# Moving weight conversions, key norms and block reads to other pieces of the first period of a DeltaNet + maxout-FFN kernel

## The chip, the cores and the metric

The kernel runs on one core of a Trainium2 chip. The metric is the device time of one execution in microseconds (us), lower is better. A core has a matrix engine (PE, with its weight loads listed as PEld), a vector engine (DVE), a scalar engine (ACT), a general engine (POOL) and SP, which here only issues DMA transfers. Each engine works through its own instruction list strictly in order and waits on semaphores for the others.

## The reference

Two blocks follow each other. The first is a DeltaNet recurrence over 768 tokens for 4 batches and 8 heads of 48 dimensions; the second is a feed-forward block whose hidden layer is the maximum of three projections.

```python
k_n = k / (np.linalg.norm(k, axis=-1, keepdims=True) + 1e-06)
for t in range(S):
    kt, vt, bt = (k_n[:, :, t], v[:, :, t], beta[:, :, t, None])
    y[:, :, t] = np.einsum('bhd,bhde->bhe', q[:, :, t], state)
    v_old = np.einsum('bhde,bhd->bhe', state, kt)
    state = state + bt[:, :, :, None] * np.einsum('bhd,bhe->bhde', kt, vt - v_old)
...
x = y.transpose(0, 2, 1, 3).reshape(B * S, H * D)          # 3072 x 384
h = np.maximum(np.maximum(x @ w1, x @ w2), x @ w3)         # 3072 x 768
return h @ w_out                                           # 3072 x 384
```

Everything is float32 at the outside; the inputs of the weights arrive as 64-bit floats, which the kernel reads as pairs of 32-bit words and turns into float32 itself.

## The kernel before

**Tiling.** The recurrence is done in 12 chunks `c` of 64 tokens. A *unit* `n = 2c + g` is one chunk for two of the four batches. Two chunks make a *period* `m` (4 units, 512 rows of x); there are 6 periods. Per unit, `turn` (L330) transposes keys and queries on PE (`p_t`) and copies them to `kqt`; `gram` (L400) multiplies keys by keys and by queries (`p_g`), of which DVE takes the masked query part `pt` (L395) and ACT the key part `at` (L428); `to_dram` (L432) writes `at` to DRAM (`at_d`). `blocks(m)` (L461) reads a period's four sets of 32x32 diagonal blocks back from DRAM with four DMAs (L471), so that each partition holds one whole block (`x_bl`; for period 1 it lies inside the tile `wo_sb`).

**The triangular solve.** `solve(m)` (L481) is a generator that runs almost wholly on DVE: it clears `y_bl` (L489), scales by the key norms (`norm`, L243, and L493 to L505) and then does column after column of an elimination, each one product (L519, `tmp`) and one subtraction (L523, `y_bl`). For periods 0 and 1 there are 15 columns of 16x16 blocks, later 31 columns of 32x32 blocks. Then it stores the result to DRAM (L528, `y_d`) and reads it back into `ut` (L537). Each resumption (`some(solving, k)`) does k columns. The chunk recurrence follows: `halves_t`/`halves_z`/`halves_u` (`p_e`, `p_f`), `join_z`/`join_u` (`p_z`, `p_j`), `old_k`/`old_q`, `new` (`p_u`), `step` (`p_s`, state `st` at L731), `to_y` and `to_x` (`p_x`, then the copy into `xt`, L805 to L808).

**Norms of the values.** `prep_sums(c)` (L260) squares the keys on ACT (L267), sums them on DVE (L268) and swaps halves with two small DMAs (L273). `prep_values(c)` (L282) turns the sums into norms (one square root on ACT, L245, five small DVE instructions, L246 to L250) and scales `v_t` on POOL (L277).

**Weights.** There are 24 slabs: 18 of w1 to w3 (in the order in which the hidden pieces need them) and 6 of w_out. `fetch` (L188) queues a slab's DMA (L192) into one of 5 `w_bits` buffers. One call of `some(conv, 1)` converts: ACT takes `mant` (L211) and `up` (L220) of a new slab, POOL clamps `mant` (L215), and the slab of the call before is joined: DVE L230 and L234, then a POOL addition (L238) into `w_sb` or `wo_sb`. `mant` and `up` have two buffers each. The same five buffers later hold `turned`, the keys and queries that `load_blocks` (L358) brings straight from DRAM.

**The feed-forward generator.** `ffn(m)` (L811) yields after each *piece*. In period 0, pieces 0 to 8 are the first 256 columns of hidden rows 0 to 2, pieces 9 to 17 the other 256 columns, pieces 18 to 26 hidden rows 3 to 5 with 512 columns, each 3 matmuls into `p_h` (2 PSUM buffers) and one take-over: piece 0, 3, 6, ... by ACT (L830), the two others by DVE (L832, `h`). Pieces 27 to 30 are the outputs `p_o`, copied by ACT (L854) and stored by SP (L857). Piece i needs the buffer of piece i-2 to be free. PE work of the recurrence shares three PSUM buffers in turn (`ps_two`).

**Order.** Nothing is scheduled by a planner: within `manual_schedule` each engine's list is the order in which the Python code calls. The loop at L1019 goes through the pieces of `ffn(0)`, and after each piece emits the rest of period 0 (`FIRST`), the work on period 1 (`EARLY_LINKS`), conversions (`CONVERTED`), loads, norms, and the solves of periods 1 and 2. Later periods use the loop at L1060. DMAs go to SP's queue in the same order; one whose data or buffer isn't ready holds up all behind it.

Of the kernel before, what the change touches and what calls it, by code (L numbers as in the profile page):

```python
# [21 lines left out]
def kernel(  # L22
# [31 lines left out]
    nc = tc.nc  # L54
# [47 lines left out]
    one_queue = (nc.sync, nc.sync)  # L102
# [355 lines left out]
    def in_blocks(t):  # L458
        return t[:, :, 0 : HB * BL].rearrange("p s (j i) -> p s j i", i=BL)

    def blocks(m, queues=one_queue):  # L461
        if m == 1:
            xs[m] = in_wo(0)
        else:
            xs[m] = work.tile([128, 2, HB * BL + HB], FP32, name="x_bl", bufs=1)
        x = in_rows(xs[m])
        for half in range(2):
            part = slice(BL * half, BL * (half + 1))
            for cc in range(2):
                p0 = 64 * half + 32 * cc  # L470
                queues[cc].dma_start(  # L471
                    out=x[p0 : p0 + 32],
                    in_=at_d[m][cc, part, :, :, part].rearrange(
                        "j b h i -> (b h) j i"
                    ),
                )
# [4 lines left out]
    def solve(m):  # L481
# [3 lines left out]
        if m == 1:  # L485
            y_bl = in_wo(1)
        else:
            y_bl = work.tile([128, 2, HB * BL + HB], FP32, name="y_bl", bufs=1)
            (nc.vector if m else nc.gpsimd).memset(y_bl, 0.0)  # L489
        y = in_rows(y_bl)  # L490
        bl = small("bl", BL)
        norm(bl, diagonal(x), small("root_bl", BL), small("nt_bl", BL))
# [83 lines left out]
    fine = {}  # L576
# [23 lines left out]
        return slice(hs[0], hs[-1] + 1)  # L600

    def halves_z(c):
        if c not in fine:
            halves_t(c)
        at = [ats[2 * c + g] for g in range(2)]
        second = ut[c % NU].rearrange("p g h (f two x) -> p g h f two x", two=2, x=HB)
        for hs, p_v, copy in heads_of(c, "p_e", BL):
            for i, h in enumerate(hs):
                for bb, g in TILES:
                    r = rows(bb)  # L610
                    nc.tensor.matmul(
                        p_v[rows(bb ^ g), g, i], at[g][r, h], second[r, g, h, :, 1]
                    )
            copy(zs[c % NU][:, :, span(hs)], p_v)
# [247 lines left out]
    def some(gen, n):  # L862
        for _ in range(n):
            if next(gen, gen) is gen:
                break
# [86 lines left out]
    halves_z(1)  # L952
    load_q(3)
    to_x(0)
    for n in range(2):
        some(conv, 1)
        fetch(nc.sync)
    load_q(4)
    load_v(2)
    solving = solve(1)  # L960
    some(solving, 2)

# [50 lines left out]

    CONVERTED = {4, 5, 6, 7, 8, 10, 12, 14, 16, *range(17, 27)}
    for i, _ in enumerate(ffn(0)):  # L1019
        if i > 4 and i - 1 in CONVERTED:  # L1020
            fetch(nc.sync)
        queries(FIRST.get(i, ""))
        links(1, EARLY_LINKS.get(i, ""))
        if i in CONVERTED:
            some(conv, 1)
        if i in (1, 2):
            prep_sums(i + 1)
        if i in (4, 5):
            some(solving, 4 if i == 4 else 2)
        if i in (5, 7):  # L1030
            prep_values(i // 2)
        if i in (5, 6, 9, 10):
            load_k(i + 3 - i // 9 * 2)
        if i == 0:
            load_v(3)
        if i == 12:
            load_q(11)
        if i in (15, 18):
            load_v(4 + i // 18)
        if i == 19:  # L1040
            blocks(2)
            prep_sums(4)
        if i == 20:
            solving = solve(2)
            some(solving, 1)
        if i > 20:
            some(solving, 3 if i < 29 else 4)
        if i == 21:
            prep_values(4)
        if i == 22:  # L1050
            prep_sums(5)
        if i == 24:
            prep_values(5)
        if i in (27, 28):
            load_blocks(i - 15)

# [47 lines left out]
```

## Time and profile before

| | |
|---|---|
| median of 4 runs | 591.69 us (590.99 to 592.17) |
| profiled execution: own time, span | 592.17 us, 590.5 us |
| granted PE clock, mean over the span | 0.948 |
| PE busy | 543.1 us (92%), 8106 matmuls |
| DVE busy | 348.0 us (59%), 778 instructions |
| ACT busy, POOL busy | 140.3 us (24%), 119.0 us (20%) |
| chain that ended last, by engine | PE 61%, DVE 13%, DMA 10%, SP queue 6% |

The profile is of one execution, the slowest of the four shown. "Busy" is an average over stages with different limits, so the stage that the change touches has to be read by itself. Pieces 0 to 30 of `ffn(0)` lie between 61.3 us and 194.5 us of the span: piece 9 starts at 99.4, piece 18 at 132.6, piece 27 at 176.4. In a row of the timeline the numbers are start and duration in us, then engine, line, instruction, output and inputs, count, and in brackets the idle time of the engine before it and what ended it.

### The profile page before, as it was taken

What the parts mean: (1) busy time and instruction counts of PE and PEld (TensorE: products, weight loads), DVE (VectorE), ACT (ScalarE), POOL (GpSimd) and SP (SyncE); (2) the same over time, 40 slices, a digit from 0 to 9 for tenths busy, and PEclk for the clock granted to TensorE, in tenths of its full rate; (3) what the DMA queues carried; (4) which work ended last, traced back from release to release, by engine and by line L of the source; (5) the groups of instructions that cost most, each with busy time, mean ns of one, the idle gap of its engine ahead of it and who ended that gap; (6) DMA issues with size and microseconds to landing.
All of it is one profiled execution on the core that took longest, in us unless ns stands there. A gap on an engine that the chain in (4) does not pass through costs nothing.

```text
span 590.5 us, 18712 instructions
## 1 busy us (share of the span) xinstructions
PE 543.1 (92%) x8106; PEld 318.7 (54%) x8106; DVE 348.0 (59%) x778; ACT 140.3 (24%) x274; POOL 119.0 (20%) x209
## 2 busy tenths in 40 slices
PE   6468699999869999999999999999999999999997
PEld 5337577775435545555555455455455455554443
DVE  1648879766799453899554898555895432201110
ACT  3326336545311122112121112121111211010000
POOL 6024206213326423002802004600001000000000
PEclk9556779999998999999999999999999999999999
DMA  9998916967204654264754644833744101210002
GB/s 159 154 173 227 195 25 137 190 156 157 47 2 116 145 117 101 73 118 95 185 120 82 115 90 109 190 86 73 119 101 92 17 2 54 68 40 1 0 0 53
DMA packets 159505, 58.76 MB, mean 100 GB/s; under 512 B 141184, under 2 KB 153280, under 8 KB 159424
## 3 DMA queue, kind: packets, MB, share of 16 engines
q1 hardware_dynamic: 150736, 51.58, 42.8%
q0 software_dynamic: 3200, 4.82, 3.5%
q10 hardware_dynamic: 5488, 1.18, 1.2%
q8 instruction: 63, 1.03, 0.8%
q14 instruction: 18, 0.15, 0.1%
HBM read 40.21 MB, written 17.30 MB: 97 GB/s over the span
## 4 chain that ended last, share of the span: by engine, by line
PE 61%; DVE 13%; DMA 10%; SPq 6%; issue 3%; ACT 3%; POOL 2%; ACTq 0%; DVEq 0%; POOLq 0%
PE p_h L822 38%; PE p_o L846 9%; DVE y_bl L523 3%; PE p_g L411 3%; DMA y_d<-y_bl 3%; DMA kpad<-in_k_dram 3%; DVE tmp L519 2%; SPq L369 2%; PE p_u L703 2%; PE p_k L675 1%; PE p_t L339 1%; PE p_j L658 1%; DMA ut<-y_d 1%; SPq L115 1%; PE p_q L675 1%
## 5 line engine op out<-in xcount | busy, mean ns | idle before, releaser
L822 PE MATMUL p_h<-xt,w_sb 128*128 128x512 f32 (+1 forms) x702 | 303.8, 577 | 7.0 <-ACT h L830 2.8
L822 PEld LDWEIGHTS p_h<-xt,w_sb 128*128 128x128 f32 x702 | 129.3, 193 | 129.9 <-issue 116.0
L832 DVE TENSOR_TENSOR h<-h,p_h 128x512 f32<-128x512 f32 (+1 forms) x78 | 50.1, 642 | 94.4 <-PE p_h L822 93.7
L846 PE MATMUL p_o<-wo_sb,h 128*128 128x384 f32 x288 | 96.1, 494 | 3.8 <-DVE h L832 3.8
L846 PEld LDWEIGHTS p_o<-wo_sb,h 128*128 128x128 f32 x288 | 55.2, 193 | 42.1 <-issue 6.0
L523 DVE TENSOR_TENSOR y_bl<-y_bl,tmp 128x31 f32<-128x31 f32 (+20 forms) x139 | 57.7, 415 | 4.8
L277 POOL TENSOR_TENSOR v_t<-v_t,nrm 128x768 f32<-128x768 f32 x12 | 17.7, 1474 | 193.3 <-DVE nrm L250 165.1
L369 POOL DMA_DIRECT2D turned<-in_q_dram x96 | 52.1, 550 | 4.2 <-POOL turned L364 3.8
L519 DVE TENSOR_TENSOR tmp<-x_bl,y_bl 128x31 f32<-128x31 f32 (+20 forms) x139 | 47.3, 340 | 3.7
L830 ACT COPY h<-p_h 128x512 f32<-128x512 f32 (+1 forms) x39 | 21.5, 552 | 106.2 <-PE p_h L822 106.2
L411 PE MATMUL p_g<-kqt 48*64 48x64 f32 (+1 forms) x1280 | 34.2, 250 | 10.4 <-ACT kqt L345 5.7
L411 PEld LDWEIGHTS p_g<-kqt 48*64 48x64 f32 x1280 | 28.5, 148 | 19.5 <-ACT kqt L345 7.9
L854 ACT COPY o_sb<-p_o 128x384 f32<-128x384 f32 x24 | 11.5, 478 | 91.4 <-PE p_o L846 80.1
L215 POOL TENSOR_SCALAR mant<-mant 128x384 f32<-128x384 f32 x24 | 12.5, 520 | 72.1 <-ACT mant L211 71.4
L428 ACT COPY at<-p_g 128x512 f32<-128x512 f32 x21 | 12.3, 585 | 45.3 <-DVE pt L395 40.1
L395 DVE TENSOR_TENSOR pt<-p_g,mask 128x512 f32<-128x512 f32 x22 | 15.2, 690 | 10.3 <-PE p_g L411 10.1
L385 DVE STREAM_TRANSPOSE kqt<-turned 128x256 f32<-128x256 f32 x48 | 17.3, 415 | 4.9 <-DMA turned<-in_k_dram 4.7
L238 POOL TENSOR_TENSOR w_sb<-mant,up 128x384 int32<-128x384 int32 x18 | 18.0, 999 | 5.5 <-DVE mant L234 5.5
L618 DVE TENSOR_SCALAR ut<-p_j 32x512 f32<-32x512 f32 (+1 forms) x13 | 8.3, 647 | 17.6 <-ACT ut L620 17.6
L703 PEld LDWEIGHTS p_u<-v_t,ut 64*64 64x64 f32 x768 | 13.4, 142 | 8.4 <-issue 5.1
L731 DVE TENSOR_TENSOR st<-st,p_s 128x768 f32<-128x768 f32 x11 | 10.5, 950 | 12.4 <-PE p_s L725 12.3
L675 PEld LDWEIGHTS p_k<-st,kqt 48*64 48x64 f32 x704 | 12.0, 140 | 9.9 <-issue 6.9
(111 smaller groups left out, 488.9 us busy)
## 6 DMA issues: line engine op xcount, KB each, us to landing
w_bits<-in_moe_w_dram SPq DMA_DIRECT2D x18, 384.0 KB
at_d<-at SPq DMA_DIRECT2D x45, 128.0 KB
v_t<-in_v_dram SPq DMA_DIRECT2D x24, 192.0 KB
turned<-in_q_dram POOLq DMA_DIRECT2D x96, 48.0 KB, 3.2
out_dram<-o_sb SPq DMA_DIRECT2D x48, 96.0 KB
turned<-in_k_dram SPq DMA_DIRECT2D x96, 48.0 KB
kpad<-in_k_dram SPq DMA_DIRECT2D x44, 96.0 KB
y_x<-y SPq DMA_DIRECT2D x16, 192.0 KB
```

Source lines behind the costliest of these rows:

```text
L238: nc.gpsimd.tensor_tensor(out=dst.bitcast(I32), in0=mant_v.bitcast(I32), in1=up_v, op=ALU.add)
L277: nc.gpsimd.tensor_tensor(out=vts[c], in0=vts[c], in1=nrm[:, :, :, None].to_broadcast([128, 2, H, D]), op=ALU.mult,)
L369: (nc.sync, nc.gpsimd)[i].dma_start(out=t[p0 : p0 + 32, bb, at : at + NP * 2 * D].rearrange("p (j x) -> p j x", j=NP), in_=(k, q)[i][2 * b ...
L411: nc.tensor.matmul(p_g[rows(bb ^ (g * i)), par, c0 : c0 + C * (1 + whole)], kq[:, 0], kq if whole else kq[:, i],)
L519: nc.vector.tensor_tensor(out=t_v, in0=row.to_broadcast(t_v.shape), in1=column.to_broadcast(t_v.shape), op=ALU.mult,)
L523: nc.vector.tensor_tensor(out=rest, in0=rest, in1=t_v, op=ALU.subtract)
L675: nc.tensor.matmul(p_b[rows(bb), par, c0 : c0 + D], kqt[g][dims(par), j, bb ^ g, i], st[dims(par), bb ^ g, g, j],)
L703: nc.tensor.matmul(p_v[rows(bb ^ g), g, i], ut[c % NU][rows(bb), g, h], rhs[rows(bb), g, h],)
L822: nc.tensor.matmul(p_h, w_sb[i][:, t, f * 128 : (f + 1) * 128], xt[:, t, lo : lo + w], start=(t == 0), stop=(t == KT - 1),)
L830: nc.scalar.copy(h, p_h)
L832: nc.vector.tensor_tensor(out=h, in0=h, in1=p_h, op=ALU.max)
L846: nc.tensor.matmul(p_o, hs[f][:, i * 128 : (i + 1) * 128], wo_sb[:, f], start=(f == 0), stop=(f == FT - 1),)
```

## The change

Only the order of work before and during `ffn(0)` is changed, and one engine.

- Two weight conversions and two fetches that stood ahead of the loop are gone from there, and so is one of the two resumptions of `solve(1)`. The 19 conversion calls in the loop (pieces 4 to 8, 10, 12, 14, 16, 17 to 26) become 20 (2 to 8, 10, 12 to 23). The last slab is joined at piece 22 and not 24; each fetch still stands one piece behind a conversion.
- `halves_t(1)`, three DVE transposes (L583, L585), is no longer called in `halves_z(1)` ahead of `to_x(0)` but behind it. So DVE's half of the copy into `xt` (L808) now precedes them.
- `solve(1)` does 4, 2 and 1 steps at pieces 4, 5 and 6 and not 4 and 2 at 4 and 5: its store moves from piece 4 to 5 and its second reload to piece 6.
- Key loads for units 8 to 11 move from pieces 5, 6, 9, 10 to 7 to 10; a load of v from piece 15 to 10.
- The sums for chunks 4 and 5 move from pieces 19 and 22 to 11 and 15, their norms from 21 and 24 to 14 and 20.
- `blocks(2)` is issued in two parts: chunk 0's two DMAs at piece 16, chunk 1's two at piece 18, and not all four at 19.
- `solve(2)` starts at piece 21 and not 20, does 3 steps at pieces 22 to 26, 4 at 27 to 29 and 5 at 30 (before: 3 at 21 to 28, 4 at 29 and 30). Its `y_bl` is cleared by POOL and not by DVE.

```diff
-    def blocks(m, queues=one_queue):
+    def blocks(m, queues=one_queue, chunks=(0, 1)):
         if m == 1:
             xs[m] = in_wo(0)
-        else:
+        elif m not in xs:
             xs[m] = work.tile([128, 2, HB * BL + HB], FP32, name="x_bl", bufs=1)
...
-            for cc in range(2):
+            for cc in chunks:
...
-            (nc.vector if m else nc.gpsimd).memset(y_bl, 0.0)
+            (nc.vector if m > 2 else nc.gpsimd).memset(y_bl, 0.0)
...
     def halves_z(c):
-        if c not in fine:
+        if c > 1:
             halves_t(c)
...
     to_x(0)
-    for n in range(2):
-        some(conv, 1)
-        fetch(nc.sync)
+    halves_t(1)
     load_q(4)
     load_v(2)
     solving = solve(1)
-    some(solving, 2)
+    some(solving, 1)
...
-    CONVERTED = {4, 5, 6, 7, 8, 10, 12, 14, 16, *range(17, 27)}
+    CONVERTED = {*range(2, 9), 10, *range(12, 24)}
     for i, _ in enumerate(ffn(0)):
-        if i > 4 and i - 1 in CONVERTED:
+        if i - 1 in CONVERTED:
             fetch(nc.sync)
...
-        if i in (4, 5):
-            some(solving, 4 if i == 4 else 2)
+        if i in (4, 5, 6):
+            some(solving, (4, 2, 1)[i - 4])
         if i in (5, 7):
             prep_values(i // 2)
-        if i in (5, 6, 9, 10):
-            load_k(i + 3 - i // 9 * 2)
+        if 7 <= i < 11:
+            load_k(i + 1)
...
-        if i in (15, 18):
+        if i in (10, 18):
             load_v(4 + i // 18)
-        if i == 19:
-            blocks(2)
-            prep_sums(4)
-        if i == 20:
+        if i in (11, 15):
+            prep_sums(4 + i // 15)
+        if i in (14, 20):
+            prep_values(4 + i // 20)
+        if i in (16, 18):
+            blocks(2, chunks=(i // 18,))
+        if i == 21:
             solving = solve(2)
             some(solving, 1)
-        if i > 20:
-            some(solving, 3 if i < 29 else 4)
-        if i == 21:
-            prep_values(4)
-        if i == 22:
-            prep_sums(5)
-        if i == 24:
-            prep_values(5)
+        if 21 < i < 27:
+            some(solving, 3)
+        if i >= 27:
+            some(solving, 4 if i < 30 else 5)
         if i in (27, 28):
             load_blocks(i - 15)
```

## The prediction

> **What bounds the kernel now.** First I read the table of slices, then the waits of PE by stretch, then the timeline of PE and DVE side by side. In the slices, 40 of 14.8 us each:
>
> ```profile
> PE   6468699999869999999999999999999999999997
> DVE  1648879766799453899554898555895432201110
> PEclk9556779999998999999999999999999999999999
> ```
>
> Beyond slice 14 PE is full; what can be had lies in the first 13. The change touches slices 4 to 13. Busy times there by stretch (engine, busy us, instructions; then granted clock, DMA share and GB/s):
>
> ```profile
> 66.80:82.00 15.20, 10.85 (x246) 8.77 (x245) 11.46 (x30) 4.67 (x12) 0.00 (x0) 0.66 0.82 106
> 82.00:97.00 15.00, 14.46 (x367) 11.84 (x366) 13.80 (x38) 8.40 (x18) 5.00 (x6) 1.00 0.39 88
> 97.00:111.00 14.00, 14.00 (x363) 11.63 (x361) 13.25 (x25) 7.84 (x15) 7.03 (x8) 1.00 0.75 159
> 111.00:132.50 21.50, 19.44 (x599) 16.11 (x599) 13.60 (x28) 10.39 (x21) 3.58 (x6) 1.00 0.83 164
> 146.00:176.40 30.40, 23.28 (x302) 11.90 (x298) 26.35 (x63) 7.67 (x17) 8.61 (x10) 0.94 0.16 29
> ```
>
> The reader is to see three kinds of stretch: DVE full from 82 to 111 (27.05 of 29 us), DVE with room from 111 to 132.5 (13.6 of 21.5), and DVE full again from 146 to 176 (26.35 of 30.4) while PE loses 7 us. PE's waits, first from 57 to 97, then from 145 to 200:
>
> ```profile
> PE p_z L645 <- DVE ut L618: 1.8, 1, 1.8
> ...
> PE p_x L757 <- DVE st L731: 0.5, 1, 0.5
> ```
>
> ```profile
> PE p_o L846 <- DVE h L832: 3.8, 1, 3.8
> PE p_h L822 <- DVE h L832: 2.6, 2, 1.9
> PE p_h L822 <- ACT h L830: 0.7, 1, 0.7
> ```
>
> So in the second place PE stands for DVE's take-over of the hidden pieces, which waits in DVE's list behind the solve, conversions and norms. Two rows of PE show that a stall costs twice, for the next matmuls run at half clock (2.84 and 7.91 us are what the same rows take undisturbed); the DVE rows show a step of the solve beside a POOL addition and the next one without:
>
> ```profile
> 159.89 4.51 PE L822 MATMUL p_h<-xt,w_sb 128*128 128x512 f32 x6 [1.93 <-DVE h L832]
> ...
> 176.43 9.67 PE L846 MATMUL p_o<-wo_sb,h 128*128 128x384 f32 x24 [3.78 <-DVE h L832]
> ```
>
> ```profile
> 161.97 0.99 DVE L523 TENSOR_TENSOR y_bl<-y_bl,tmp 128x112 f32<-128x112 f32 x1
> 162.99 0.30 DVE L519 TENSOR_TENSOR tmp<-x_bl,y_bl 128x135 f32<-128x135 f32 x1
> ```
>
> **The change part by part.** PE's own list is the same before and after; only its waits can move. All times are places in the old trace.
>
> *1. The start of the loop (58 to 97).* DVE's copy of `xt` stood behind three transposes (58.60 to 60.75) and ended at 61.19. Ahead of them it still waits for ACT's half (to 60.27), so it ends at 60.3 + 0.52 = 60.8: 0.4 us. The transposes then end near 63.0, ahead of their reader `p_f` at 63.8. Two joins (61.22 to 63.71, 2.5 us) leave DVE, and with them the ACT conversion that held `root_bl` until 64.47. The norm of `solve(1)` can start at 63.0 and, as its first step took 0.97 beside POOL where 0.18 is usual, takes 2.85 and not 3.6 us. Then the second L618 ends at 67.5 (before 69.96), `p_z` starts at 67.9 (70.11) and `p_k` at 68.6 (71.09): 2.5 us won by PE.
>
> It does not keep them. The two joins (1.9 us) come back at pieces 2 and 3, and one solve column (0.45) comes behind that L618, in a stretch where DVE is the bound. From the first L618 (68.67) to the end of `st` (95.63) DVE was busy 23.5 us and waited 3.5. Now it starts at 66.15, has 23.5 + 1.9 + 0.45 = 25.85 us of work, and I find 2.4 us of waits left (0.44 for ACT's half of L618, 0.6 for squares, 1.3 for `p_j`): `st` ends at 94.4. Adding 0.6 for one more POOL addition beside it (0.99 against 0.30 above) gives 95.0. `p_x`, which takes over the PSUM buffer that `st` frees, gains 0.6 to 1.2; I take 0.9. From `st` to 111 DVE's list is unchanged and full, so 0.9 is what arrives at 111. Bounds: 2.5 (all kept) and -1.7: PE now stands some 2 us in small pieces between 87 and 95, and 1.93 us of standing ahead of 159.89 was followed by 1.67 of half clock.
>
> The Trainium skill's "TensorE: Matmul & The Clock Gate", in its table on why this matters, wants gaps under about 3 us for the clock to stay up; by that rule the -1.7 would be nil. The row with 1.93 decides against it here.
>
> *2. The middle (111 to 146).* DVE gets two more joins (0.95 each), chunk 4's norm (1.0) and chunk 5's sums (1.0), 3.9 us, less a clearing of 0.94; ACT gets two more conversions (1.0 each). The room is there (DVE 7.9 us from 111 to 132.5), but lists are in order. Laid out: the join of piece 13 and a `z` copy behind ACT's conversion push `pt` at 123.69 by 1.0; ACT's `at` follows that, then its conversion, a root (0.2), `h`, `z`, and `kqt`, which ends at 129.1 and not 127.56. `p_g` at 128.43 waits for it: 0.7. Squares and a conversion then precede L620/L618, and `p_t` at 131.64 finds its buffer freed 0.4 later. That is -1.1. By 140 both engines have caught up. Bounds: 0, and -5.6 if the 3.9 us are all exposed, with one spell of half clock (1.7). A gain isn't excluded: three gaps of PE put down to "issue" here, 2.1 us in all, may go, for the loads move too.
>
> *3. The wait for DVE (146 to 186).* Of four joins behind the norm (0.94, 2.09, 0.95, 0.95) one is left (0.95); chunk 5's sums (1.0) and two norms (1.05, 1.07) leave; and five solve steps that ran 0.7 to 0.95 us too long beside POOL (0.94 for 0.22, 0.99 for 0.26, 1.02 for 0.33, 1.08 for 0.38, 1.37 for 0.42) have one POOL addition left beside them. DVE loses 7.1 us of work and some 3 of slowing (3.8 less one 0.7). In the new order, with the norm at 151.95 (below), `h` of piece 22 comes at 155.2 (before 159.06), needed by PE at 157.3; piece 23's at 159.1, needed at 161.1; piece 25's ends at 165.65, needed at 167.7; piece 26's at 169.0, needed at 171. `h` of piece 21 no longer stands on ACT behind `root_bl`. All four waits go: 0.73 + 1.93 + 0.71 + 3.78 = 7.15, and with them the half clock, 4.51 - 2.84 = 1.67 and 9.67 - 7.91 = 1.76 (stall inside `p_o` included). Together 10.6. Bounds: 10.6, and 5.0 if piece 23's margin of 2 us fails and one stall with half clock stays, or two of 1 us.
>
> *4. Blocks by chunk.* Four L471 issues took 6.62 us of SP behind unit 11's `at_d`; now two (3.3) precede it, which with a pair of L273 (1.2) and two fetches (1.3) makes `at_d` 1.2 later, and two follow. `x_bl` lands near 150.5 (151.1), but ACT's `root_bl` now stands behind `qs` and a conversion, so the norm starts at 151.95 (151.48). I cost it at nothing: DVE has `h` and joins until 149.95. If chunk 0's issues stood for data, at worst another 3.3 us on `solve(2)`, whose end has 1.2 to spare (5). The other SP moves, key loads behind fetches, land near 107.4 (issue end 102.6 plus the 4.8 that the chain shows at 28.83) for `p_t` at 108.7: 0, at worst 0.7.
>
> *5. The end of `solve(2)`.* It matters, for `p_z` at 213.93 already waits 0.69 for `ut`. Before, columns ended at 193.34, but SP issued the store at 196.31, behind the output of piece 30 (`p_o` ends 194.5). After: 169.9, plus 2.7 for three columns, plus 12.1 for 16 (181.23 to 193.34): 184.8, against `p_o` ending at 184.1 and the store's turn at 186. So the store follows PE still, and the gain passes on. Lost cover costs one for one.
>
> *6. Clearing by POOL.* It takes 0.94 from DVE at 148.08, where DVE waited afterwards: nothing. By the Trainium skill's "SBUF — State Buffer", section on who interferes with whom, a POOL instruction that only writes doesn't block DVE's two-input steps; no row of this trace has such a pair, and a reading one cost 0.7.
>
> **Sum.** 0.9 - 1.1 + 10.6 = 10.4. Against the profiled execution's own 592.17: 581.8. The median of the runs is 0.5 lower; I leave that inside the scatter.
>
> **The rivals.**
>
> *Half of it (20%).* DVE stays the bound from 146 on: `h` of piece 23 or 25 comes 2 us late, a stall and a half-clock spell stay, or the solve ends 3 to 5 us behind the store's turn. For it: DVE is still over 80% full there. Against: the margins in 3 are all over 1 us. 5 us less: 587.
>
> *No change (5%).* The gain is handed back at `p_z`, because `ut` is late. For: the wait is there now. Against: SP's store follows PE. It needs columns that end 11 us after 184.8. 592.
>
> *Slower (12%).* ACT stands at L211 for POOL's addition of two slabs earlier, which stands for a DVE join; with eight conversions at pieces 12 to 19, each holds up the copies of `z`, `kqt` and `ut` that PE waits for next. For it: ACT waits this way 12.4 us in all before, up to 3.3 at a time. Against: only 21.4 of 35 us of ACT are used. It decides from 10.4 / 8 = 1.3 us per conversion, on top of the 1.1 in part 2; at 1.7 the time is 595.
>
> *More (3%).* The 2.3 us gap at 72.85 and the "issue" gaps go too: 577.
>
> **How the numbers follow.** The forecast, 578 to 586, has 60%. The range reaches to most of the half case: 578 to 589.5. A change of 0.2% is 1.2 us, about what a measurement of this kernel can tell. Faster: 60 + 20 + 3 = 83%; same 5%; slower 12%.
>
> **What would show it.** Right: no wait of PE for `h` between 146 and 186, clock 1.0 there; `p_x` near 95 and `p_z` near 68; waits near 129 of about 1 us; the store of `y_d` right behind piece 30's output. Wrong: `kqt` or `z` over 2 us late near 129, or `p_z` after the loop waiting several us for `ut`.

## The result and the profile after

The changed kernel takes 589.25 us (median of 33 runs, 584.16 to 594.78) beside 592.49 us for the kernel before on the same chips: a ratio of 0.9936, 95% interval 0.9918 to 0.9954. It is faster by 0.64%, 3 to 4 us, where 10.4 us were forecast. The profiled execution has an own time of 589.13 us and a span of 587.4 us (before: 592.17 and 590.5).

The three lines of the slices, of the kernel after:

```profile
PE   6358797979999999999999999899999999999997
DVE  1548789776899553898554897455895422301110
PEclk9556789998999999999999999899999999999999
```

The dip of PE in the eleventh and twelfth digits (148 to 177 us) is gone, so the place at which most of the gain was forecast did change. Now the busy times by stretch, of the kernel after (start:end, length; busy us and instructions of PE, weight loads, DVE, ACT, POOL; granted clock, DMA share, GB/s):

```profile
66.80:82.00 15.20, 13.21 (x349) 10.80 (x348) 11.88 (x31) 5.97 (x13) 0.51 (x1) 0.78 0.36 61
82.00:97.00 15.00, 10.75 (x258) 8.45 (x257) 14.31 (x34) 7.57 (x16) 6.68 (x8) 1.00 0.56 136
97.00:111.00 14.00, 13.32 (x360) 11.13 (x360) 12.92 (x25) 7.00 (x14) 7.38 (x10) 1.00 0.83 166
111.00:132.50 21.50, 17.05 (x502) 14.13 (x499) 15.35 (x33) 11.48 (x25) 5.18 (x8) 1.00 0.76 162
146.00:176.40 30.40, 29.93 (x504) 16.84 (x504) 26.66 (x57) 6.90 (x14) 18.25 (x31) 1.00 0.29 59
```

Read the PE column against the one before. From 146 to 176 us PE is busy 29.93 us (before 23.28) at a clock of 1.00 (0.94). From 66.8 to 82 it is busy 13.21 us where it was 10.85, work that comes sooner. But from 82 to 97 it is busy 10.75 us where it was 14.46, and from 111 to 132.5 17.05 where it was 19.44: time that came in at the end went out in front. PE's waits, of the kernel after, from 57 to 97 us (first fence), 97 to 145 (second) and 145 to 200 (third); total us, times, longest:

```profile
PE p_g L411 <- DVE y L745: 2.1, 1, 2.1
...
PE p_x L757 <- DVE st L731: 1.1, 1, 1.1
```

```profile
PE p_g L411 <- DVE z L649: 2.7, 1, 2.7
...
PE p_t L339 <- DMA kpad<-in_k_dram: 0.6, 2, 0.5
```

```profile
PE p_h L822 <- DVE h L832: 0.5, 1, 0.5
```

The wait of `p_z` for `ut` (1.8) is gone, and of 7.1 us of waiting behind 145 us one of 0.5 is left. New is a wait of `p_g` for the copy `z`, and behind it two rows at half clock (1.10 and 1.56 us are what they take undisturbed):

```profile
132.94 1.74 PE L411 MATMUL p_g<-kqt 48*64 48x128 f32 x32 [2.65 <-DVE z L649]
134.61 2.56 PE L822 MATMUL p_h<-xt,w_sb 128*128 128x256 f32 x6
```

The two PE rows that stood at half clock before are these in the kernel after (start, us, engine):

```profile
159.81 2.84 PE L822 MATMUL p_h<-xt,w_sb 128*128 128x512 f32 x6
...
174.05 8.01 PE L846 MATMUL p_o<-wo_sb,h 128*128 128x384 f32 x24
```

2.84 and 8.01 us against 4.51 and 9.67: full clock, no wait. And the solve step that took 0.99 us beside POOL, with the step behind it:

```profile
167.42 0.28 DVE L523 TENSOR_TENSOR y_bl<-y_bl,tmp 128x112 f32<-128x112 f32 x1
167.73 0.30 DVE L519 TENSOR_TENSOR tmp<-x_bl,y_bl 128x135 f32<-128x135 f32 x1
```

From PE's timelines I cut the span at three marks: the first `p_x` of the loop, the start of `p_h` of piece 18 (the first piece 512 tokens wide), and the end of `p_o` of piece 30. Lengths in us:

| stretch | before | after | gain | forecast |
|---|---|---|---|---|
| start to `p_x` | 95.69 | 96.62 | -0.93 | +0.9 |
| `p_x` to `p_h`(18) | 36.88 | 42.10 | -5.22 | -1.1 (and part 4: 0) |
| `p_h`(18) to end of `p_o`(30) | 61.95 | 51.76 | +10.19 | +10.6 |
| from there to the end | 395.98 | 396.92 | -0.94 | 0 |
| sum | 590.5 | 587.4 | +3.1 | +10.4 |

So the question is not why DVE's wait stayed (it went) but what took 6 us away in front of it. In the middle stretch, from `p_x` to `p_h`(18), PE's own rows account for 5.0 of the 5.2 us: its waits sum to 5.5 us where they were 2.1, and the two rows at half clock take 1.6 us more.

### The profile page after: what moved, and what is told of

The parts are those of the page before. It is cut to its first block, busy times and chain, and to the rows that moved or that the text cites. A ratio compares the mean times of both kernels' runs of the same rounds, so it can differ in the third digit from the quotient of the medians.

```text
span 587.4 us, 18714 instructions
## 1 busy us (share of the span) xinstructions
PE 541.9 (92%) x8106; PEld 318.5 (54%) x8106; DVE 348.6 (59%) x777; ACT 139.4 (24%) x274; POOL 120.0 (20%) x210
## 4 chain that ended last, share of the span: by engine, by line
PE 69%; DVE 11%; DMA 9%; issue 3%; SPq 3%; ACT 3%; POOL 1%; ACTq 0%; DVEq 0%; POOLq 0%
PE p_h L822 42%; PE p_o L846 11%; DMA kpad<-in_k_dram 4%; PE p_g L411 4%; DVE tmp L519 2%; DVE y_bl L523 2%; PE p_y L743 2%; PE p_k L675 2%; DMA turned<-in_q_dram 2%; PE p_u L703 2%; PE p_s L725 1%; SPq L115 1%; PE p_q L675 1%; PE p_j L658 1%; PE p_t L339 1%
## 5 line engine op out<-in xcount | busy, mean ns | idle before, releaser
L846 PE MATMUL p_o<-wo_sb,h 128*128 128x384 f32 x288 | 94.4, 487 | 0.0
L523 DVE TENSOR_TENSOR y_bl<-y_bl,tmp 128x31 f32<-128x31 f32 (+20 forms) x139 | 54.9, 395 | 4.8
L267 ACT ACTIVATE ksq<-kpad 128x384 f32<-128x384 f32 x20 | 9.9, 519 | 31.8 <-DMA kpad<-in_k_dram 31.5
```

The costliest lines, as they stand in the source:

```text
L523: nc.vector.tensor_tensor(out=rest, in0=rest, in1=t_v, op=ALU.subtract)
L846: nc.tensor.matmul(p_o, hs[f][:, i * 128 : (i + 1) * 128], wo_sb[:, f], start=(f == 0), stop=(f == FT - 1),)
```

## The experiments

DVE's own timeline gave the theories. Of the kernel after:

```profile
113.28 0.55 DVE L268 TENSOR_REDUCE ksum<-ksq 128x8 f32<-128x384 f32 x1 [0.48 <-ACT ksq L267]
116.08 0.55 DVE L268 TENSOR_REDUCE kflip<-ksq 128x8 f32<-128x384 f32 x1 [2.25 <-ACT ksq L267]
...
117.26 0.42 DVE L618 TENSOR_SCALAR ut<-p_f 16x256 f32<-16x256 f32 x1
...
130.17 0.99 DVE L246 TENSOR_SCALAR newton<-root 128x16 f32<-128x16 f32 x1 [0.80 <-ACT root L245]
...
132.11 0.69 DVE L649 COPY z<-p_z 32x512 f32<-32x512 f32 x1
```

What DVE's reduction stood for, on ACT:

```profile
115.52 0.52 ACT L267 ACTIVATE ksq<-kpad 128x384 f32<-128x384 f32 x1 [2.28 <-DMA kpad<-in_k_dram]
```

The same two steps, `ut` and `z`, of the kernel before:

```profile
113.68 0.42 DVE L618 TENSOR_SCALAR ut<-p_f 16x256 f32<-16x256 f32 x1 [1.17 <-ACT ut L620]
...
126.64 0.69 DVE L649 COPY z<-p_z 32x512 f32<-32x512 f32 x1 [1.41 <-ACT z L648]
```

Where DVE stood 1.4 us behind the old trace ahead of the sums (`t` of L585 at 111.37 against 109.94), it is 3.6 us behind at `ut`: chunk 4's sums, moved to piece 11, made ACT and DVE stand for a key tile that SyncE had issued only at 109.56. At `z` it is 5.5 us behind: ACT's conversion of piece 13 in front of the first `z` (4.1 behind there) and chunk 4's norm, 130.17 to 132.1 with its wait, in front of the second (1.3 more). Theory K names the late keys, theory N the norm, theory C the conversions of pieces 13 and 15, theory F the two conversions taken from ahead of the loop. Below, e0 to e15 name the runs, and "the middle" is the stretch from `p_x` to `p_h`(18).

**Each part by itself on the changed kernel.** Norm of chunk 4 three pieces later (e1):

```diff
-        if i in (14, 20):
+        if i in (17, 20):
             prep_values(4 + i // 20)
```

> The changed kernel with one edit: the norm of chunk 4's keys runs behind piece 17 and not behind piece 14. The changed kernel profiles at 589.1 us. Theory N (the norm of chunk 4 stands on VectorE from 130.17 to 132.11 in front of the copy z, for which the matmuls p_g wait 2.65 us at 132.94, and the stall brings TensorE to half clock for one stretch): p_g starts at about 131.8, when kqt is there, that is 1.1 us sooner, and without the half-clock stretch another 1.6 us come back: about 586.5 us, and no wait for z over 1.6 us. Theory K (the chain is late because the square of chunk 4's keys waits 2.28 us at 115.52 for keys loaded late): VectorE is at the copy z sooner but all before it is as late as it was, so at most the norm's own 1.3 us: 588 us. If neither holds: 589 us.

Measured: 587.46 us, ratio 0.9878 (0.9833 to 0.9923). `p_h`(18) comes 39.63 us behind `p_x` (42.10). DVE's copy `z` of this kernel, and the PE rows that follow from it:

```profile
130.94 0.69 DVE L649 COPY z<-p_z 32x512 f32<-32x512 f32 x1 [1.42 <-ACT z L648]
```

```profile
131.91 1.10 PE L411 MATMUL p_g<-kqt 48*64 48x128 f32 x32
132.94 1.56 PE L822 MATMUL p_h<-xt,w_sb 128*128 128x256 f32 x6
```

The wait for `z` is gone and the clock whole: what N said; the time lies between N's 586.5 us and K's 588. DVE's wait ahead of the reduction (2.2 us) stayed, as K leaves it.

Key loads where they were (e2):

```diff
-        if 7 <= i < 11:
-            load_k(i + 1)
+        if i in (5, 6, 9, 10):
+            load_k(i + 3 - i // 9 * 2)
```

> The changed kernel with one edit: the four key loads stand behind pieces 5, 6, 9 and 10 as in the kernel before, not behind 7 to 10. Theory K: ScalarE no longer waits 2.28 us for kpad at 115.52, VectorE's reduction no longer idles 2.25 us, and PE's two waits for kpad (0.6 us) go: the first copies ut move from 117.26 to about 115.1, and p_h(18) from 138.7 to about 136: about 586.5 us. Theory N: the waits for kpad go, but the norm still stands in front of the copy z and the half-clock stretch stays: 588.5 us. A third theory (the queue's order costs only PE's own 0.6 us of waits): 588.5 us.

Measured: 586.45 us, ratio 0.9841 (0.9784 to 0.9898). DVE's rows of this kernel:

```profile
114.02 0.55 DVE L268 TENSOR_REDUCE ksum<-ksq 128x8 f32<-128x384 f32 x1
114.49 0.54 DVE L268 TENSOR_REDUCE kflip<-ksq 128x8 f32<-128x384 f32 x1
...
116.35 0.42 DVE L618 TENSOR_SCALAR ut<-p_f 16x256 f32<-16x256 f32 x1 [0.72 <-ACT ut L620]
```

The 2.25 us are gone and no wait for keys is left on PE; but PE still waits 2.0 us for `z` behind the norm, and `p_h`(18) gains only 1.4 us on `p_x` in this profile. PE's rows of this kernel at that wait:

```profile
132.36 1.10 PE L411 MATMUL p_g<-kqt 48*64 48x128 f32 x32 [2.00 <-DVE z L649]
133.39 1.56 PE L822 MATMUL p_h<-xt,w_sb 128*128 128x256 f32 x6
```

The clock stays whole here, and from this `p_g` to `p_h`(18) it takes 4.80 us where the changed kernel takes 5.78. So 1.0 of the 1.4 us is half clock that isn't there, and only 0.4 is a `z` that comes sooner behind `p_x`. The time is better than the profile explains; its interval is almost 7 us wide.

The two conversions ahead of the loop again (e3):

```diff
+    for n in range(2):
+        some(conv, 1)
+        fetch(nc.sync)
     halves_t(1)
...
-    CONVERTED = {*range(2, 9), 10, *range(12, 24)}
+    CONVERTED = {*range(4, 9), 10, *range(12, 24)}
...
-        if i - 1 in CONVERTED:
+        if i > 4 and i - 1 in CONVERTED:
```

> The changed kernel with one edit: the two weight conversions that the change moved from ahead of the loop to pieces 2 and 3 are ahead of the loop again, behind the first copy of x and ahead of the second chunk's transposes. Theory F (beside the two conversions VectorE's norm steps are slow between 82 and 95 us, which costs the 1.8 us between the forecast start of p_x, 94.8, and its start, 96.6): p_h(6) no longer waits 1.1 us for a slab, p_x starts near 95, and the 1.8 us reach the end: 587.3 us. Its rival (the two conversions cost VectorE ahead of the loop what they cost it in the loop; p_z goes from 68.4 back to near 70): 589 to 590 us.

Measured: 589.73 us, ratio 0.9920 (0.9886 to 0.9953). `p_h`(6) no longer waits for a slab and `p_x` starts at 94.86, as F said; `p_z` falls back to 71.76. But the 1.8 us that F saw reach the end don't show: the time can't be told from the changed kernel's.

No conversions behind pieces 13 and 15 (e4):

```diff
-    CONVERTED = {*range(2, 9), 10, *range(12, 24)}
+    CONVERTED = {*range(2, 9), 10, 12, 14, *range(16, 25)}
```

> The changed kernel with one edit: no weight conversion behind pieces 13 and 15; two more run behind pieces 23 and 24. Theory C (the conversions put between pieces 13 and 16 hold ScalarE for 1.1 us each in front of the copies z, which come at 125.14 and 130.30, and VectorE for 0.9 us each): both copies come 1 to 2 us sooner, p_g waits about 1 us instead of 2.65 and the clock stays full: minus 1.5 to 3 us in the middle, plus at most 1.2 us behind piece 22, where VectorE has 1.9 us more to do: 587 us. Theories N and K: the norm still ends at 132 or the keys still land at 115.5, and the two conversions cost VectorE again later: 589 to 590 us.

Measured: 591.38 us, ratio 0.9956 (0.9924 to 0.9987). The middle is 0.8 us shorter than in the changed kernel (41.30), less than two profiles of one kernel differ by (e0, below), with 1.8 us left of the wait for `z`; the two conversions at 23 and 24 bring back a wait behind 146 us, of this kernel:

```profile
PE p_o L846 <- DVE h L832: 2.3, 1, 2.3
```

**Both edits together (e5), and what else could be put right.** "Both edits" are the later norm and the early key loads:

```diff
-        if 7 <= i < 11:
-            load_k(i + 1)
+        if i in (5, 6, 9, 10):
+            load_k(i + 3 - i // 9 * 2)
...
-        if i in (14, 20):
+        if i in (17, 20):
             prep_values(4 + i // 20)
```

> The changed kernel with both edits: the norm of chunk 4 behind piece 17, and the four key loads behind pieces 5, 6, 9 and 10. If the two delays are links of one chain (the late square holds VectorE's copies ut for 2.15 us, and behind it the norm holds the copy z for 1.3 us), both come back, and the half-clock stretch behind the wait for z with them: 2.15 + 1.3 + 1.6 = 5.0 us under the changed kernel, a ratio to the kernel before of about 0.985. If each edit alone already removes the one stall that costs time, both together are no better than the better one alone, 2 to 3 us under the changed kernel: 0.989. No wait of PE over 1 us is left between 126 and 146 us but the gaps named issue.

Measured: 584.27 us, ratio 0.9848 (0.9796 to 0.9901); the profiled execution has an own time of 582.15 us, a span of 580.4. PE's waits of this kernel from 97 to 146 us:

```profile
PE p_g L411 <- issue: 1.0, 2, 0.8
PE p_g L411 <- ACT kqt L345: 0.8, 1, 0.8
PE p_f L628 <- issue: 0.6, 1, 0.6
PE p_t L339 <- DVE ut L618: 0.3, 1, 0.3
```

No wait for `z` or keys; `p_h`(18) comes 37.55 us behind `p_x` (before 36.88) and the end of `p_o`(30) 51.76 us behind that. This profile is within 0.4 us of the forecast of 581.8 us, in part by luck (its `p_x`, at 94.16, lies at the early end of the scatter shown below); the median is 2.5 us above it. And the ratio's interval lies below that of the changed kernel (0.9918 to 0.9954).

The conversions of 13 and 15 moved to 11 and 23, on top of both edits (e6). (In the changed kernel the call behind piece 23 is empty, since the last slab is joined at 22; with one call less in front it does the last join.)

```diff
-    CONVERTED = {*range(2, 9), 10, *range(12, 24)}
+    CONVERTED = {*range(2, 9), 10, 11, 12, 14, *range(16, 24)}
```

> As the kernel with both edits, and the conversions behind pieces 13 and 15 moved to pieces 11 and 23. If the conversion behind piece 13 holds the copy z on ScalarE (0.9 us at 124.24 to 125.14), the two z copies and all behind them come 0.9 us sooner: 0.5 to 1 us under the kernel with both edits. If the conversion at piece 11 puts the same 0.9 us in front of the copies ut of pieces 12 and 13, nothing is gained; and with a conversion at piece 23 in a stretch where VectorE was the bound, up to 1 us is lost: 0 to 1 us over it.

Measured: 585.59 us, ratio 0.9873 (0.9825 to 0.9922): no better. Behind 146 us the conversion at piece 23 costs 0.9 us (52.62 against 51.76), as the second case had it. The middle is 40.37 us long in this profile, but PE's gaps named issue sum to 4.1 us there (1.6 with both edits), so what the 0.9 us of ACT are worth was not decided.

Conversions where the kernel before has them, the rest as with both edits (e8):

```diff
-    CONVERTED = {*range(2, 9), 10, *range(12, 24)}
+    CONVERTED = {4, 5, 6, 7, 8, 10, 12, 14, 16, *range(17, 27)}
...
+    for n in range(2):
+        some(conv, 1)
+        fetch(nc.sync)
     halves_t(1)
```

> As the kernel with both edits, but with the conversions where the kernel before has them: two ahead of the loop, then behind pieces 4 to 8, 10, 12, 14, 16 and 17 to 26; sums, norms, blocks and solve(2) stay where the change puts them. If the conversions behind pieces 23 to 26 alone hold VectorE in the stretch from 146 to 186 us (4 x 1.9 us of steps, slowed beside GpSimd's part), most of the 10.6 us forecast come back as waits for h and the y store: 591 to 594 us, PE waits over 5 us in all there. If it is the norms and sums that the change took out of that stretch, most of the gain stays: 586 to 588 us, PE waits under 3 us there.

Measured: 585.89 us, ratio 0.9889 (0.9842 to 0.9937). The middle takes 35.97 us, the shortest of all; behind it 56.01 us (51.76 with the conversions moved, 61.95 before). The waits, of this kernel from 146 to 200 us:

```profile
PE p_o L846 <- DVE h L832: 2.3, 1, 2.3
PE p_h L822 <- DVE h L832: 0.7, 2, 0.5
```

So conversions are 4.25 of the 10.2 us won there; the other 6 belong to sums, norms, blocks and the solve's place (sums and norms alone: 4.0, below). And of what the conversions win behind, they give part back in the middle, where the kernel with both edits takes 1.6 us longer, and two more that are alike there (e11 and e7, below) 3.1 and 3.7.

The changed kernel itself once more (e0):

> The changed kernel once more, beside the others on the same chip: a ratio to the kernel before near 0.994. If the starts of the work up to 97 us (p_x at 96.6 in its profile, p_z at 68.5) move by a microsecond or more in another profile of the same kernel, then the 0.9 us read as lost in the first stretch are scatter of the run; if they stay within 0.3 us, they belong to the change.

Measured: 589.00 us, ratio 0.9950 (0.9915 to 0.9985). `p_z` at 68.40 and `p_x` at 96.45, within 0.2 us, and the wait for `z` is again 2.65 us. But the middle takes 44.23 us where the first profile has 42.10: `z` comes 1.0 us later behind `p_x`, and the half clock behind the wait lasts longer. PE's rows of this second profile:

```profile
133.74 1.99 PE L411 MATMUL p_g<-kqt 48*64 48x128 f32 x32 [2.65 <-DVE z L649]
135.66 2.93 PE L822 MATMUL p_h<-xt,w_sb 128*128 128x256 f32 x6
```

From this `p_g` to `p_h`(18) it takes 6.94 us, against 5.78 in the first profile and 4.80 at full clock in e2, which has the same lists from there on. So the half clock did cost time: 1.0 us in one profile, 2.1 in the other. In front, three other kernels that run the same list up to there (e1, e4, and e9 below) start `p_x` at 96.72, 94.94 and 97.75. A single profile thus carries up to 3 us of scatter in front and 2 in the middle.

**Which step of the chain holds what.** Sums behind piece 13 and the norm later, keys still late (e9):

```diff
-        if i in (11, 15):
-            prep_sums(4 + i // 15)
+        if i in (13, 15):
+            prep_sums(4 + i // 15)
...
-        if i in (14, 20):
+        if i in (17, 20):
```

> The changed kernel with two edits: the norm of chunk 4 behind piece 17, and chunk 4's squares and sums behind piece 13 and not behind piece 11; the key loads stay late, behind pieces 7 to 10. If ScalarE and VectorE standing at the square for late keys is what the early key loads took away, the delay goes here too: no 2.2 us of idle time before the reduction, the first copies ut near 115.3 instead of 117.3, and only PE's 0.5 us for kpad stay: 1 us over the kernel with both edits, a ratio near 0.987. If the place of the four loads in SyncE's queue is what counts, and not the square, this kernel is no better than the one with the norm alone: 0.988 to 0.991, and copies ut at 117.

Measured: 589.74 us, ratio 0.9928 (0.9888 to 0.9969). The wait of 2.2 us is gone, and `ut` comes 19.2 us behind `p_x` instead of 20.6. But the squares (0.92 us on ACT) now stand in front of the copy `z`, and the reduction waits 1.1 us: `p_h`(18) is 39.74 us behind `p_x`, no better than with the norm alone (39.63). Moving the consumer only moved the cost; the expected gain didn't come.

Matmuls nobody reads, in the stall ahead of `p_g` (e10):

```diff
-        14: "z0 d1 g1", 15: "z1 t2", 16: "j0 g2", 17: "j1 t3", 18: "u0 g3", 19: "s0",
+        14: "z0 d1 g1", 15: "z1 t2", 16: "j0 b0 g2", 17: "j1 t3", 18: "u0 g3", 19: "s0",
...
+            elif f == "b":
+                busy(14, ident)
```

> The changed kernel with one addition: 14 matmuls of the identity by itself, whose result nobody reads, stand between p_j and the matmuls p_g that wait 2.65 us for z; at 0.15 us each (6 of p_x took 0.95 us) they fill 2.2 us of the stall. If the stall itself brings the clock down, p_g takes 1.1 us again instead of 1.74 and the next six p_h 1.56 instead of 2.56: 1.6 us back, p_h(18) near 137.1, a ratio of about 0.991. If the half-clock stretch comes from something else than TensorE standing, it stays: 0.9936 as the changed kernel.

Measured: 589.13 us, ratio 0.9935 (0.9899 to 0.9972). PE's rows of this kernel:

```profile
130.12 3.39 PE L877 MATMUL p_w<-ident 128*128 128x128 f32 x28 [0.18 <-ACT h L830]
133.44 1.10 PE L411 MATMUL p_g<-kqt 48*64 48x128 f32 x32
135.79 1.56 PE L822 MATMUL p_h<-xt,w_sb 128*128 128x256 f32 x6 [1.25 <-DVE h L832]
```

The clock stayed whole (1.10 and 1.56 us, not 1.74 and 2.56), as it should if the standing brought it down, though e2 kept it behind a wait of 2.00 us as well. Nothing came back: `p_h`(18) starts at 138.90 (138.72). But that is the filler's own doing. Its output takes one of the two PSUM buffers that the `p_h` take in turn:

```python
def busy(n, of):
    p_w = ps_ffn([128, TOK], "p_w")[:, 0 : of.shape[1]]
    ...
```

So `p_h` of piece 17 now needs the buffer of piece 16 and waits 1.25 us for its `h`, which DVE reaches at 135.32. In the changed kernel the same `p_h` needs the buffer of piece 15 and starts at 134.61, a microsecond ahead of that `h` (135.63). So this run doesn't tell what the half clock costs; e2 and the second profile of the changed kernel do.

Blocks read whole, with both edits (e11):

```diff
-        if i in (16, 18):
-            blocks(2, chunks=(i // 18,))
+        if i == 18:
+            blocks(2)
```

> The kernel with both edits, but the blocks of the second period are read whole behind piece 18 instead of chunk by chunk behind 16 and 18. The forecast costed this part at nothing: if that is right, the time is that of the kernel with both edits within its interval (0.985), and solve(2) begins at the same place. If the earlier read of the first chunk is what lets solve(2) begin behind piece 21, its first step waits for x, and what stands behind it on VectorE (h, z) with it: 1 to 2 us over.

Measured: 587.14 us, ratio 0.9883 (0.9827 to 0.9940). From `p_h`(18) to `p_o`(30) it takes 51.76 us, to the hundredth the same as with both edits; the times' intervals overlap. Reading by chunks moves nothing there.

Both edits and the two conversions ahead of the loop (e7):

```diff
+    for n in range(2):
+        some(conv, 1)
+        fetch(nc.sync)
     halves_t(1)
...
-    CONVERTED = {*range(2, 9), 10, *range(12, 24)}
+    CONVERTED = {*range(4, 9), 10, *range(12, 24)}
...
-        if 7 <= i < 11:
-            load_k(i + 1)
+        if i in (5, 6, 9, 10):
+            load_k(i + 3 - i // 9 * 2)
...
-        if i in (14, 20):
+        if i in (17, 20):
```

> The kernel with both edits, and the two conversions of pieces 2 and 3 ahead of the loop again. The kernel with the late conversions had its p_h(18) at 130.2, 1.5 us before the kernel with both edits, but lost it again in the stretch behind (a wait of p_o for h of 2.3 us). If its early start is owed to these two conversions, this kernel keeps it and has no such wait: 1.5 us under the kernel with both edits, 0.982. If it is owed to the conversions missing at pieces 13 and 15, or is scatter, this kernel equals the one with both edits: 0.985.

Measured: 584.99 us, ratio 0.9847 (0.9789 to 0.9905), the same as both edits. `p_h`(18) is 39.70 us behind `p_x`, so the short middle of the kernel with the late conversions was not owed to these two. Whether it was owed to the conversions missing at pieces 13 and 15 or is scatter stays open: e5, e11 and this kernel, alike in the middle but for the block reads, take 37.55, 39.04 and 39.70 us.

**Four corners on the kernel before.** Since single edits and both had overlapping intervals, I took the conversions out of the question. Late keys alone (e12):

```diff
-        if i in (5, 6, 9, 10):
-            load_k(i + 3 - i // 9 * 2)
+        if 7 <= i < 11:
+            load_k(i + 1)
```

> The kernel before with one part of the change alone: the four key loads behind pieces 7 to 10. In this kernel the squares of chunk 4 come only behind piece 19. If late keys cost only where a square of ScalarE stands for them, PE's waits for kpad grow by 0.6 us and no more: 592.5 to 593.5 us, a ratio of 1.000 to 1.002. If the place of the loads on SyncE's queue costs by itself, 2 us or more are lost: 1.004 or above.

Measured: 594.89 us, ratio 1.0025 (0.9987 to 1.0064). The wait, of this kernel:

```profile
PE p_t L339 <- DMA kpad<-in_k_dram: 2.2, 1, 2.2
```

With no square in front, PE itself stands 2.2 us for the keys of unit 8, where 0.6 were expected; the middle is 2.4 us longer. The time lies between the two cases, at a difference that its interval doesn't tell from none.

Sums and norms alone (e13):

```diff
-        if i in (15, 18):
+        if i in (10, 18):
             load_v(4 + i // 18)
+        if i in (11, 15):
+            prep_sums(4 + i // 15)
+        if i in (14, 20):
+            prep_values(4 + i // 20)
...
-            prep_sums(4)
-        if i == 21:
-            prep_values(4)
-        if i == 22:
-            prep_sums(5)
-        if i == 24:
-            prep_values(5)
```

> The kernel before with the sums and norms alone where the change puts them (sums behind pieces 11 and 15, norms behind 14 and 20, the values of chunk 4 loaded behind piece 10); key loads, conversions, blocks and solve(2) as before. The kernel with the late conversions kept about 6 of the 10 us behind 146 us, so 6 us come there; the norm in front of the copy z takes 1.5 to 2 back: 588 us, a ratio of 0.992, and p_g waits 1 to 2 us for z near 130. If the norm in front of z costs nothing without the conversions of pieces 13 and 15: 586.5 us, 0.990.

Measured: 591.76 us, ratio 0.9941 (0.9902 to 0.9980). Behind 146 us 4.0 us are won (57.97 against 61.95). `p_g` waits 1.6 us for `z`, yet the middle takes 36.76 us, as before: the gaps named issue are 0.8 us here and were 2.1.

The same with late keys (e14):

```diff
-        if i in (5, 6, 9, 10):
-            load_k(i + 3 - i // 9 * 2)
+        if 7 <= i < 11:
+            load_k(i + 1)
```

> As the kernel with the norms alone, and the key loads late, behind pieces 7 to 10: now ScalarE's square of chunk 4 stands for keys behind piece 11, without any conversion moved. If late keys and an early square together are the cause, 1.5 to 2.5 us over the kernel with the norms alone (0.995 to 0.996), with 2 us of idle time of VectorE ahead of the reduction; if the keys alone did it, the same as what they cost the kernel before; if neither, no difference.

Measured: 590.63 us, ratio 0.9935 (0.9898 to 0.9971). DVE's waits of this kernel from 104 to 146 us, and PE's from 97 to 146:

```profile
DVE ksum L268 <- ACT ksq L267: 1.9, 1, 1.9
DVE kflip L268 <- ACT ksq L267: 1.9, 1, 1.9
```

```profile
PE p_t L339 <- DMA kpad<-in_k_dram: 1.9, 1, 1.9
```

The middle is 3.6 us longer (40.32). The times don't show it: same ratio.

The norms alone, with chunk 4's behind piece 17 (e15), against e13:

```diff
-        if i in (14, 20):
+        if i in (17, 20):
             prep_values(4 + i // 20)
```

> As the kernel with the norms alone, but the norm of chunk 4 behind piece 17 instead of 14. If the norm in front of the copy z is a cost by itself: 1.3 to 2 us under the kernel with the norms alone, 0.989, and no wait of p_g for z over 1 us. If it only costs together with the moved conversions and late keys: the same as with the norms alone, 0.992.

Measured: 590.46 us, ratio 0.9915 (0.9875 to 0.9956). No wait for `z`, but gaps named issue (3.1 us in all), and the middle at 38.62 us: nothing won by the profile, 0.0026 by the times, inside both intervals.

**What holds over all of them.** Pairs that differ in one thing, by the length of the middle in their profiles and by their ratios ("after" is the changed kernel's first profile):

| difference | pairs | middle, us | ratio |
|---|---|---|---|
| keys late, not early | before/e12, e13/e14, e2/after, e5/e1 | +2.4, +3.6, +1.4, +2.1 | +0.0025, -0.0006, +0.0095, +0.0030 |
| norm behind 14, not 17, conversions moved | e1/after, e5/e2 | +2.5, +3.1 | +0.0058, -0.0007 |
| norm behind 14, not 17, conversions as before | e15/e13 | -1.9 | +0.0026 |

Each length is of one profile, and two profiles of one kernel lay 2.1 us apart. Late keys lengthen the middle in all four pairs, 2.4 us in the mean; their ratios have a mean of +0.0036, 2.1 us, though one pair shows nothing. The norm lengthens the middle by 2.5 to 3.1 us where the moved conversions are in the list too, and not in the one pair where they aren't; one of its ratios shows nothing. How the 6 us split between the two stays open: most of the single kernels' intervals are 4 to 7 us wide. That both together were most of the loss is shown: the three kernels with both edits (e5, e11 with the blocks whole, e7 with two conversions ahead of the loop) have ratios of 0.9848, 0.9883 and 0.9847, against 0.9936 and 0.9950 of the changed kernel, 3 to 6 us, and neither the wait for `z` nor one for keys.

## Why the prediction was wrong, point by point

**Part 3, the wait for DVE: right.** +10.19 against +10.6, the clock at 1.00. One wait of 0.47 us for `h` is left, and part 6 explains it (below). That PE came 6 us late did not help it: with both edits `p_h`(18) starts at 131.71, as early as in the old trace, and the stretch takes the same 51.76 us. Its mechanism splits as 4.25 us for the conversions and 6 for the rest.

**Part 2, the middle: the step that failed.** It was costed at -1.1 and it came to -5.2 with part 4's keys (-7.35 in the second profile). The list of added work was right (two joins, norm, sums, two conversions). What failed is "By 140 both engines have caught up" together with the steps laid out: the norm was taken as 1.0 us of DVE, but with its wait for ACT's root, and the first step at 0.99 beside POOL, it holds DVE from 129.4 (its idle time included) to 132.1, directly in front of the copy that frees `p_g`'s PSUM buffer. I had looked for a late `kqt`; `kqt` was there at 131.8, `z` at 132.8. My bound of -5.6 held it, for the reason given there (the 3.9 us all exposed), but the value taken was the optimistic end. The spell of half clock in that bound was there too; of its 1.6 us in PE's rows 1.0 reached `p_h`(18), by the comparison with e2.

**Part 4, key loads: mis-sized.** "0, at worst 0.7" rests on a landing of the first key tile at 107.4, from an issue that ends at 102.6. SP came to it later, behind a reload of `ut`, a slab and queries: the issue ended at 106.4 (105.5 in e12), and the tile was there at 110.7 (109.2). So late keys cost by themselves: in e12, where nothing else is moved, PE's `p_t` stands 2.2 us. The second tile was issued at 109.56 (104.93 with the loads early), and for it the change had put a new reader ahead: chunk 4's squares, moved to piece 11, stood on ACT for it, and DVE behind ACT, while PE, late already, waited 0.5 us. Late keys cost 2.4 us of the middle in the mean, three times the worst case. For the blocks by chunk, nothing was right.

**Part 1, the start: right at `p_z`, wrong in sign at `p_x`.** `p_z` at 68.45 was forecast at 67.9. Over all profiles, `p_f` to `p_z` takes 4.5 us in the ten with the two conversions moved and 6.6 in the eight without: 2.1 us won, 2.5 forecast. But `p_f` to `p_x` takes 32.3 and 30.6: 1.7 us lost, where 0.9 were to be left. The copy of `xt` ahead of the transposes has no part in it: the three kernels with that copy moved but the conversions ahead of the loop need 30.9 us, the five with neither 30.4. The bound of -1.7 was met; the reason differs: `p_h`(6) waits for the very slab that was converted late (1.1 us), and DVE's steps beside POOL, whose busy time from 82 to 97 went from 5.00 to 6.68 us, are slow more often than the one addition I allowed for. Six of them ran 2.8 us over in all (two, 1.0 us, before), and behind them in DVE's list stand the `y` and the `st` for which `p_g` and `p_x` wait 2.1 and 1.1 us.

**Part 5, the end of `solve(2)`: right.** Its columns end at 191.44 and the store goes out at 192.26, behind piece 30's output at 190.5.

**Part 6, clearing by POOL: not quite nothing.** POOL's rows of the kernel after, then DVE's:

```profile
157.94 0.98 POOL L238 TENSOR_TENSOR wo_sb<-mant,up 128x384 int32<-128x384 int32 x1
158.87 0.97 POOL L489 MEMSET y_bl<- 128x1056 f32 x1
```

```profile
157.99 1.89 DVE L246 TENSOR_SCALAR nt_bl<-root_bl 128x32 f32<-128x32 f32 x1 [0.38 <-ACT root_bl L245]
```

A step of 0.18 us beside nothing took 1.89 and ended when the clearing ended; it stands in front of the `h` for which PE waits 0.47 us. In all 13 profiles with the clearing on POOL this step takes 1.88 to 1.91 us, in the five without it 0.18. The Trainium skill's "SBUF — State Buffer", section on who interferes with whom, counts `tensor_scalar` among the steps that can take the port pair shared with GpSimd, and says that whichever has the pair then blocks the other fully; I had used only its sentence on two-input steps. The row agrees with the former.

**From there to the end.** 0.94 us went in one profile, with a half-clock spell between 371 and 377 that the old trace lacks; over the 18 profiles this length varies from 394.9 to 401.0 us, so I put no cause to it.

**The rivals.** Not one named what happened. Slower had the right place (copies `z`, `kqt`, `ut` held up by added work in front of them) with the wrong holder: conversions standing for POOL, where it was the norm and a square standing for keys. Half of it put the loss behind 146 us, where there was none. The forecast's sign that it would be wrong, "`kqt` or `z` over 2 us late near 129", is what the trace shows.

## What to carry to other kernels

When work is moved forward out of a full stretch into one with room, the room says little: write down, for every engine that issues in order, which copy that frees a buffer stands right behind each moved step, and what the moved step itself waits for in its new place. When a change moves a load later, read its place in the issuing queue behind everything that now precedes it, and look for its first reader over all engines, among them consumers that the same change moves earlier. And before a stall is filled with work nobody reads, see which buffer that work takes: here it took one that the next matmuls needed, and the filled stall came back as their wait.

## What the runs showed of the hardware that was not expected

A gap of PE that no wait explains is followed by half clock in the profile of one kernel and not in that of another. Kernel with the norm later, then the kernel after, the same gap in the same place:

```profile
124.45 0.79 PE L411 MATMUL p_g<-kqt 48*64 48x64 f32 x34 [1.54 <-issue]
125.17 2.93 PE L822 MATMUL p_h<-xt,w_sb 128*128 128x256 f32 x6
```

```profile
124.32 0.79 PE L411 MATMUL p_g<-kqt 48*64 48x64 f32 x34 [1.56 <-issue]
125.04 1.56 PE L822 MATMUL p_h<-xt,w_sb 128*128 128x256 f32 x6
```

1.54 us cost 1.37 us more, 1.56 us nothing; the length of the gap alone doesn't decide. Nor does it at waits with a known cause: behind 2.00 us for `z` the clock stayed whole in e2. The Trainium skill's "TensorE: Matmul & The Clock Gate" asks in its table on why this matters for gaps under about 3 us; here 1.54, 2.28 (`p_o` at 9.67 instead of 7.91 us in the kernel with the late conversions) and 2.65 us were each followed by half clock.

The gaps named issue return at the same instructions in most kernels (`p_g` behind 29 or 30 of 64 matmuls, `p_q` behind 48 of 64), with lengths from 0.2 to 2.7 us. They are part of the scatter of the middle: in the three kernels with both edits (e5, e11, e7) they sum to 1.6, 2.1 and 3.0 us, and the middle takes 37.55, 39.04 and 39.70. No run here tells what they wait for.
